# Placing the first expert slot's half steps ahead of the last routing ranks in a spectral filter and mixture-of-experts kernel

## The chip, the cores and the metric

The kernel runs on one core of a Trainium2 chip. Its time is the device time of one execution in microseconds; a median over runs is given for the kernel as a whole, and one profiled execution shows where the time goes. Engine names are those of the profile: PE (TensorE matmul) and PEld (its weight load), DVE (VectorE), ACT (ScalarE), POOL (GpSimd), SP (SyncE, which only issues DMAs here). An "ACTq" or "SPq" entry is a DMA issue by that engine's sequencer.

## The reference

Eight sequences of 2496 tokens by 256 channels are filtered in the frequency domain, and the 19968 filtered tokens go through a layer of eight experts in which each token uses one expert:

```python
X = np.fft.rfft(x, axis=1)
y = np.fft.irfft(X * (filt_r + 1j * filt_i)[None], n=2496, axis=1)    # 8 x 2496 x 256
x = y.reshape(19968, 256)
xn = x / (norm(x) + 1e-6); en = expert_emb / (norm(expert_emb) + 1e-6)
logits = xn @ en.T / tau                       # 19968 x 8
e = argmax(logits, 1); gate = softmax(logits)[e]
out = gate * (relu(x @ w1[e]) @ w2[e])         # w1: 8 x 256 x 1024, w2: 8 x 1024 x 256
```

## The kernel before

**Convolution.** Each sequence is one group. The transform of 2496 points is done as 64 by 39 with matmuls, in three stages per group: `conv_s1` (products named `s`, stored to DRAM as `SD`), `conv_s2` (loads `a` from `SD` and `f` from the filter; multiplies; product `sa`; stored as `ZD`), and `conv_sb` (product `y` from `ZD`, then the rows' logits and the routing).

**Routing.** `conv_sb` for group 0 cuts its 11 tile pairs into two chunks, of six and five. When a chunk's logits are complete, `route` runs in three parts, one per half step: part one sums the logits, part two finds the winner and the one-hot `oh`, part three computes the rank of each token within its expert by matmuls on `oh` (`rk`), adds them to the running `base`, and queues the rows' scatter to DRAM (`XS`, by indirect DMAs on POOL), sorted by expert. For group 0 alone, the first 128 rows of every expert are taken from the first chunk: the base is raised to 128 behind it, so the second chunk's rows never fall among them. The area is cleared beforehand.

**Slots.** A slot is a block of up to 256 rows of one expert. Its rows are read back from `XS` by a transposing DMA (`xTf` for the eight fixed slots of 128 rows, `xT` later), and it takes four half steps: `up(fp)` computes `ph` by 12 matmuls on PE, then ACT writes the relu `h` and DVE its low part; `down(fp)` two half steps later accumulates `po`. `read_pair(p)` reads the rows of two fixed slots, with four DMAs on SP's queue: a transposing read and a small `meta` read for each.

**Weights.** The 16 weight arrays of 1 MB are loaded by SP at the half steps in `WLOADS`. Then steps named by letter prepare each expert: `g` (sums of squares on PE, `gram`), `d` (its diagonal, DVE), `p` (sum, PE), `q` (scales, DVE), `k` (high part, ACT, line 324), `l` (low part, DVE, line 331). `WPREP` puts them at half steps of the head; `WLATE` puts the rest at the slots' own half steps, counted from 0.

**Order.** The head is one loop over half steps `n`, in which ACT, PE, DVE and SP take their instructions in the order of the program. In each step the head's own work comes first, then the weights' steps, then one slot half step if `n >= SLOTS`. For group 0, half steps 0 to 10 are `conv_s1`, 11 to 34 `conv_s2`, from 35 on `conv_sb`. The second chunk's logits end at 62, its three routing parts are at 63, 64 and 65, and its ten scatters at 65 to 69. From half step 53 on the second group's `conv_s1` runs alongside, one tile pair per half step: pair 9 at 63, pair 10, the last, at 64; its `s` products are stored by ACT's DMA queue. Behind the head the second group's `conv_s2` follows; the scheduler, which plans by a timeline of its own, may place its instructions among those of the head's last part, but behind the second chunk's new `base`, POOL's last scatter and the first `read_pair` (`behind("first")`, `behind("pl")`, `behind("read")`).

The loop itself:

```python
for n in range(HEAD):
    next(whole_head, None)
    weights(n)          # clears, read_pair(0) at FIRST_ROWS, loads, prep steps
    keep_warm(n)
    if n >= SLOTS:
        next(steps)     # one slot half step: up, late weight steps, down
```

Of the kernel before, what the change touches and what calls it, by code (L numbers as in the profile page):

```python
# [46 lines left out]
DLAG = 2  # L47
MID = 8
XNEXT = 43
WLOADS = (38, 40, 42, 44, 46, 48, 50, 52, 54, 56, 58, 60, 61, 63, 78, 79)  # L50
WPREP = {43: "g00", 44: "g01", 46: "d0", 48: "p0", 49: "q0 g10", 50: "k00", 51: "l00 k01 g11", 52: "d1 l01 k02",
# [5 lines left out]
WLATE = {16: "l52 k53 p6", 17: "l53 q6 g70", 18: "k60 g71", 19: "d7 l60 k61", 20: "l61 k62", 21: "l62 k63 p7",  # L57
         22: "l63 q7", 23: "k70", 24: "l70 k71", 25: "l71 k72", 26: "l72 k73", 27: "l73"}
SIDE = 18
CLEAR, FIRST_ROWS = 39, 64  # L60
SLOTS, HEAD = 66, 82
WARM = {-1: 8, 12: 26, 35: 22, 40: 6}
FRONT = 0
FIXED = 128
# [10 lines left out]
def moe_spectral_kernel(  # L75
# [810 lines left out]
    def read_pair(p):  # L886

        xT = mp2.tile([P, 4, 256], F16, tag="xT", name=f"xTf{p}")
        for j in range(2):
            e = 2 * p + j  # L890
            meta = mpm.tile([P, 2, 2], F32, tag="meta", name=f"metaf{e}")[:, :1]
            pairs[e] = xT[:, :, j * FIXED:(j + 1) * FIXED], meta
            at = slice(e * CAP, e * CAP + FIXED)
            read_rows(0, *pairs[e], XS16[at, 0:2 * D], XS[at, D:D + 2], fixed=True)
        last.setdefault("read", last["sp"])
# [151 lines left out]
    def weights(n):  # L1047
# [3 lines left out]
        if n == FIRST_ROWS:  # L1051
            read_pair(0)
        if n in WLOADS:
            next(loads)
# [62 lines left out]

    begun, late = [], dict(WLATE)

# [132 lines left out]
```

## Time and profile before

| | us |
|---|---|
| median of 3 runs | 1350.24 |
| lowest and highest of them | 1348.65, 1364.11 |
| the profiled execution | 1344.95 |
| its span, first to last instruction | 1343.2 |
| mean granted clock of PE | 0.970 |

The profiled execution is a little faster than the runs of the table; sums are made against its own time. Times in rows are microseconds from the span's start. A row of a timeline merges neighbouring instructions of one kind (xN). In brackets it says how long the engine was idle before, and what ended that. The releaser is inferred: the last semaphore to arrive.

### The profile page before, as it was taken

How to read it: one execution, taken by the hardware profiler on the slowest of the kernel's cores; microseconds unless marked ns; L12 is line 12 of the kernel's file. 1: busy time of each engine (PE TensorE's matmuls, PEld its weight loads, DVE VectorE, ACT ScalarE, POOL GpSimd, SP SyncE). 2: the span in 40 equal slices, each digit the busy share in tenths (PEclk: the TensorE clock that was granted, in tenths of full speed). 3: DMA queues.
4: the chain of work that ended last, by engine and by line, in shares of the span. 5: the costliest groups of instructions: out<-in, count | busy, mean ns of one | idle time of the engine just before them, and what ended most of it. 6: DMA issues, size and time to landing. Idle time of an engine off the chain costs nothing.

```text
span 1343.2 us, 36499 instructions
## 1 busy us (share of the span) xinstructions
PE 1246.3 (93%) x11027; PEld 981.2 (73%) x11027; DVE 938.8 (70%) x3078; ACT 762.2 (57%) x1760; POOL 489.2 (36%) x569
## 2 busy tenths in 40 slices
PE   7867899959897999998999999999999999999997
PEld 2344686627584778786888788878887888889886
DVE  1455796756586688976889697868786885444664
ACT  2175466825664586667757785678465843233333
POOL 0003322264255325541464346423633175111221
PEclk9997899979998999998999999999999999999999
DMA  7899868887868697868769887777675544221221
GB/s 230 271 325 369 246 185 217 186 229 226 200 169 238 190 202 174 226 192 184 168 182 245 193 195 203 224 186 194 173 196 140 119 119 106 54 49 41 57 45 37
DMA packets 272354, 241.27 MB, mean 180 GB/s; under 512 B 167123, under 2 KB 212182, under 8 KB 270373
## 3 DMA queue, kind: packets, MB, share of 16 engines
q1 hardware_dynamic: 243965, 177.87, 52.0%
q0 software_dynamic: 24320, 57.97, 14.8%
q10 hardware_dynamic: 3880, 3.03, 0.7%
q8 instruction: 104, 1.70, 0.6%
q14 instruction: 85, 0.70, 0.2%
HBM read 122.32 MB, written 85.57 MB: 155 GB/s over the span
## 4 chain that ended last, share of the span: by engine, by line
PE 71%; DMA 18%; DVE 4%; issue 3%; ACT 2%; POOL 1%; SPq 1%; ACTq 0%; DVEq 0%; POOLq 0%
PE ph L967 27%; PE po L992 26%; PE s L444 5%; DMA yT<-rows 4%; DMA f<-ZD 3%; PE sa L444 3%; PE y L444 2%; DMA f<-in_filt 2%; DMA W<-in_w 2%; PE s L439 2%; PE sa L555 2%; DMA XS<-rows,ixi 1%; DMA SD<-s 1%; PE y L439 1%; PE lp L610 1%
## 5 line engine op out<-in xcount | busy, mean ns | idle before, releaser
L992 PE MATMUL po<-W,h 128*128 (+1 forms) x3824 | 494.4, 273 | 0.2 <-ACT h L975 0.2
L967 PE MATMUL ph<-xT,wp 128*128 128x256 f16 (+2 forms) x4224 | 471.6, 258 | 10.9 <-DMA xT<-XS 3.7
L967 PEld LDWEIGHTS <-wp 128*128 128x128 f16 x4224 | 357.7, 98 | 87.8 <-issue 41.6
L992 PEld LDWEIGHTS <-h 128*128 128x128 f16 x3824 | 361.2, 98 | 68.9 <-issue 26.4
L975 ACT ACTIVATE h<-ph 128x512 f16<-128x512 f32 (+2 forms) x384 | 201.7, 527 | 244.9 <-PE ph L967 182.2
L1007 POOL DMA_INDIRECT out_dram<-o,meta x153 | 158.5, 1036 | 305.9 <-ACT o L1006 228.6
L976 DVE SCALAR_TENSOR_TENSOR h<-ph,h 128x512 f16<-128x512 f32 (+2 forms) x384 | 227.1, 591 | 48.3 <-ACT h L975 46.6
L951 DVE COPY wp<-W 128x1024 f16 x352 | 164.8, 469 | 117.8 <-PE ph L967 115.3
L790 POOL DMA_INDIRECT XS<-rows,ixi x176 | 180.1, 1023 | 142.0 <-issue 93.8
L536 POOL TENSOR_TENSOR yy<-yy,xs 128x512 f32<-128x512 f32 x60 | 80.5, 1343 | 105.6 <-DVE xs L499 85.0
L497 DVE TENSOR_TENSOR yy<-s,f 128x256 f32<-128x256 f32 x160 | 61.3, 417 | 62.5 <-ACT xs L529 27.8
L400 POOL DMA_DIRECT2D in<-in_x x66 | 38.8, 588 | 168.8 <-DVE xp L413 57.3
L635 DVE SCALAR_TENSOR_TENSOR rows<-y,rr,rows 128x256 f16<-128x256 f32 x176 | 76.7, 477 | 23.8 <-ACT rows L632 23.1
L668 ACT ACTIVATE rows<-y 128x256 f16<-128x256 f32 x176 | 67.3, 398 | 26.5 <-PE y L439 24.3
L1006 ACT ACTIVATE o<-po,meta 128x256 f32<-128x256 f32 x148 | 64.0, 478 | 28.8 <-PE po L992 27.3
L632 ACT ACTIVATE rows<-y,rr 128x256 f16<-128x256 f32 x176 | 75.5, 496 | 7.5 <-DVE rr L673 5.8
L558 ACT COPY z<-sa 128x512 f32<-128x512 f32 x80 | 46.7, 584 | 49.9 <-PE sa L555 41.2
L465 ACT COPY s<-s 128x512 f32<-128x512 f32 x88 | 52.7, 600 | 27.8 <-PE s L439 15.9
L595 ACT COPY yT<-tp 128x512 f16<-128x512 f16 x99 | 58.6, 605 | 9.1 <-PE tp L593 5.4
L444 PE MATMUL s<-xp,c1h 117*128 117x512 f32 (+1 forms) x144 | 62.0, 438 | 0.0
L412 ACT CAST yp<-yy 128x512 fp32r<-128x512 f32 x50 | 30.9, 619 | 53.0 <-POOL yy L536 52.5
L610 PEld LDWEIGHTS <-yT 128*128 128x128 f16 x704 | 33.2, 98 | 35.5 <-DMA yT<-rows 17.9
(208 smaller groups left out, 1688.8 us busy)
## 6 DMA issues: line engine op xcount, KB each, us to landing
f<-in_filt SPq DMA_DIRECT2D x160, 256.0 KB
a<-SD SPq DMA_DIRECT2D x80, 256.0 KB
ZD<-z SPq DMA_DIRECT2D x80, 256.0 KB
f<-ZD SPq DMA_DIRECT2D x80, 240.0 KB
SD<-s SPq DMA_DIRECT2D x70, 240.0 KB
in<-in_x POOLq DMA_DIRECT2D x66, 234.0 KB
W<-in_w SPq DMA_DIRECT2D x14, 1024.0 KB
in<-in_x SPq DMA_DIRECT2D x22, 234.0 KB
```

The source lines that it names most:

```text
L444: nc.tensor.matmul(out_, w[:k], b, start=(n == 0), stop=(n == 2))
L536: nc.gpsimd.tensor_tensor(out=yy, in0=yy, in1=xs, op=ALU.add)
L632: nc.scalar.activation(rows[:, i, 0:D], y[:, i], AF.Copy, scale=rr[:, u:u + 1])
L635: nc.vector.scalar_tensor_tensor(out=rows[:, i, D:2 * D], in0=y[:, i], scalar=rr[:, u:u + 1], in1=rows[:, i, 0:D], op0=ALU.mult, op1=ALU.s ...
L668: nc.scalar.activation(rows[:, i, D:2 * D], y[:, i], AF.Square, accum_out=ssq[:, u + i:u + i + 1])
L790: i = nc.gpsimd.indirect_dma_start(out=XS, out_offset=bass.IndirectOffsetOnAxis(ap=ix, axis=0), in_=src, in_offset=None)
L951: last["dve"] = nc.vector.tensor_copy(wp, src)
L967: last["pe"] = nc.tensor.matmul(ph[:, fi, :size], wp[:, k * 2 + wh, fi * P:(fi + 1) * P], xT[:, xh * 2 + k, :size], start=(c == 0), stop=( ...
L975: last["act"] = nc.scalar.activation(h[:, 0, :, :size], ph[:, :, :size], AF.Relu)
L976: last["lo"] = nc.vector.scalar_tensor_tensor(out=h[:, 1, :, :size], in0=ph[:, :, :size], scalar=0.0, in1=h[:, 0, :, :size], op0=ALU.max, ...
L992: nc.tensor.matmul(self.po[:, s], h, self.Wp[:, off + wh * 1024:off + wh * 1024 + D], start=(fp == 0 and fi == 0 and c == 0), stop=(fp == ...
L1007: i = nc.gpsimd.indirect_dma_start(out=out, out_offset=bass.IndirectOffsetOnAxis(ap=self.meta[:n, s, 0:1].bitcast(I32), axis=0), in_=o, in ...
```

## The change

Five constants and two tables. Slots' half steps begin at `n` = 63 instead of 66, the fixed rows' first read is issued at 61 instead of 64, and the head's loop ends at 79 instead of 82, so that it holds sixteen slot half steps as before. Weight loads at 60, 61 and 63 go to 59, 60 and 62, and the last two from 78 and 79 to 75 and 76. From half step 64 on the weights' steps are laid anew; the steps that no longer fall into the head open `WLATE`, which now ends at slot half step 28 instead of 27.

```diff
-WLOADS = (38, 40, 42, 44, 46, 48, 50, 52, 54, 56, 58, 60, 61, 63, 78, 79)
+WLOADS = (38, 40, 42, 44, 46, 48, 50, 52, 54, 56, 58, 59, 60, 62, 75, 76)
 WPREP = {43: "g00", 44: "g01", 46: "d0", 48: "p0", 49: "q0 g10", 50: "k00", 51: "l00 k01 g11", 52: "d1 l01 k02",
          53: "l02 k03", 54: "l03 p1 g20", 56: "q1 g21", 57: "k10", 58: "d2 l10 k11", 59: "l11 k12", 60: "l12 k13 p2",
-         61: "l13 q2 g30", 62: "k20 g31", 63: "l20", 64: "d3", 66: "k21 p3", 67: "l21 k22 q3", 68: "l22 k23 g40",
-         69: "l23 k30 g41", 70: "d4 l30 k31", 71: "l31 k32", 72: "l32 k33 p4", 73: "l33 q4 g50", 74: "k40 g51",
-         75: "d5 l40 k41", 76: "l41 k42", 77: "l42 k43 p5", 78: "l43 q5 g60", 79: "k50 g61", 80: "d6 l50 k51",
-         81: "l51 k52"}
-WLATE = {16: "l52 k53 p6", 17: "l53 q6 g70", 18: "k60 g71", 19: "d7 l60 k61", 20: "l61 k62", 21: "l62 k63 p7",
-         22: "l63 q7", 23: "k70", 24: "l70 k71", 25: "l71 k72", 26: "l72 k73", 27: "l73"}
+         61: "l13 q2 g30", 62: "k20 g31", 63: "l20", 64: "d3 k21", 65: "l21 k22 p3", 66: "l22 k23 q3", 67: "l23 g40",
+         68: "k30 g41", 69: "l30 k31 d4", 70: "l31 k32", 71: "l32 k33 p4", 72: "l33 q4 g50", 73: "k40 g51",
+         74: "d5 l40 k41", 75: "l41 k42", 76: "l42 k43 p5", 77: "l43 q5 g60", 78: "k50 g61"}
+WLATE = {16: "d6 l50 k51", 17: "l51 k52", 18: "l52 k53 p6", 19: "l53 q6 g70", 20: "k60 g71", 21: "d7 l60 k61",
+         22: "l61 k62", 23: "l62 k63 p7", 24: "l63 q7 k70", 25: "l70 k71", 26: "l71 k72", 27: "l72 k73", 28: "l73"}
-CLEAR, FIRST_ROWS = 39, 64
-SLOTS, HEAD = 66, 82
+CLEAR, FIRST_ROWS = 39, 61
+SLOTS, HEAD = 63, 79
```

## Rows read from the trace of the kernel before

**Rows 1.** The page: busy time, share of the span, instructions.
```profile
PE 1246.3 (93%) x11027; PEld 981.2 (73%) x11027; DVE 938.8 (70%) x3078; ACT 762.2 (57%) x1760; POOL 489.2 (36%) x569
```
**Rows 2.** Windows of 20 us: length, busy times, clock, DMA share, GB/s.
```profile
core 0: us, PE busy (x) PEld busy (x) DVE busy (x) ACT busy (x) POOL busy (x), PEclk, DMA share, GB/s
...
120.00:140.00 20.00, 12.59 (x78) 7.32 (x77) 10.87 (x34) 10.24 (x16) 3.52 (x3) 0.76 1.05 343
...
180.00:200.00 20.00, 20.00 (x183) 14.45 (x180) 18.34 (x63) 12.40 (x22) 4.14 (x3) 1.00 0.61 177
```
**Rows 3.** Timeline of PE, 133 to 152: start, length, what, idle time before.
```profile
133.48 2.13 PE L439 MATMUL s<-in,c_sb 117*128 117x512 f32 x6
141.03 0.23 PE L753 MATMUL rk<-oh,lt 128*128 128x80 f16 x1 [5.43 <-DVE oh L743]
...
141.85 2.72 PE L967 MATMUL ph<-xTf,W 128*128 128x128 f16 x24
...
148.66 1.93 PE L439 MATMUL s<-a,c_sb 128*128 128x512 f32 x4
150.43 0.83 PE L967 MATMUL ph<-xTf,W 128*128 128x128 f16 x12
151.10 0.82 PE L992 MATMUL po<-W,h 128*128 128x256 f16 x6
```
**Rows 4.** Small windows around the first slot, columns as in rows 2.
```profile
141.03:147.20 6.17, 5.99 (x66) 5.91 (x66) 4.62 (x20) 3.42 (x6) 2.09 (x2) 0.53 0.91 281
131.00:135.60 4.60, 4.21 (x32) 2.50 (x33) 0.92 (x4) 1.41 (x3) 0.00 (x0) 1.00 1.06 387
138.00:140.00 2.00, 0.00 (x0) 0.00 (x0) 1.73 (x4) 1.23 (x3) 0.00 (x0) 0.99 0.88 212
```
**Rows 5.** Timeline of DVE, 138 to 146.
```profile
138.20 1.28 DVE L331 SCALAR_TENSOR_TENSOR W<-W,wsc 128x1024 f16<-128x1024 f32 x1 [4.47 <-ACT W L324]
...
145.33 0.42 DVE L976 SCALAR_TENSOR_TENSOR h<-ph,h 128x256 f16<-128x256 f32 x1 [1.24 <-ACT h L975]
```
**Rows 6.** Timeline of ACT, 136 to 138.
```profile
136.65 0.32 ACTq L467 DMA_DIRECT2D SD<-s  x1
137.02 1.15 ACT L324 ACTIVATE W<-W,wsc 128x1024 f16<-128x1024 f32 x1 [3.88 <-DMA SD<-s]
```
**Rows 7.** The chain that ended last, three pieces: start, length, what.
```profile
125.71 10.87 DMA SD<-s
...
145.18 2.90 DMA a<-SD
...
295.77 3.44 DMA xT<-XS
```
**Rows 8.** SP's DMA issues, 125 to 138.
```profile
125.44 0.89 SPq L264 DMA_DIRECT2D W<-in_w  x2
130.53 1.34 SPq L878 DMA_TRANSPOSE xTf<-XS  x1
...
136.96 0.33 SPq L879 DMA_DIRECT2D metaf<-XS  x1
137.74 1.19 SPq L878 DMA_TRANSPOSE xTf<-XS  x1
```
**Rows 9.** SP's waits, 85 to 150: us in total, times, longest.
```profile
SPq L878 <- DMA XS<-rows,ixi: 4.1, 1, 4.1
...
SPq L879 <- DMA W<-in_w: 1.3, 1, 1.3
...
SPq L878 <- DMA xTf<-XS: 0.4, 1, 0.4
```
**Rows 10.** PE's waits, 140 to 225, columns as in rows 9.
```profile
PE ph L967 <- DVE h L976: 0.5, 1, 0.5
```
**Rows 11.** PE's waits, 225 to 305, columns as in rows 9.
```profile
PE s L439 <- DMA a<-SD: 6.0, 1, 6.0
PE sa L555 <- POOL yy L536: 4.7, 1, 4.7
...
PE ph L967 <- DMA xT<-XS: 1.6, 1, 1.6
```

## The prediction, made before the changed kernel was seen

> **What bounds the kernel now.** I read the page first: its busy line says that PE works 93% of the span [rows 1], so what counts is PE time: idle PE, and PE at its low clock. The windows of 20 us say where early on [rows 2]: from 120 to 140 PE is busy for 12.6 us of 20, with the DMA engines full (share 1.05, 343 GB/s) and the clock down to 0.76; from 180 to 200 it is busy for all 20 at full clock. The reader is to see two regimes: a head that lives on DMA, and, right behind it, a stretch in which PE is the limit.
>
> The first slot starts at their border, so the key view is PE's order around it [rows 3]: the last products of the head end at about 135.6, then PE stands 5.43 us for `oh`, the operand of the second chunk's rank matmuls (`rk`, 141.03), and only behind these come the first slot's `ph` matmuls (141.85). In code: half steps 63 and 64 hold the two last `s` products, 65 the ranks, 66 the first `up`. The small windows of the same place [rows 4] show the second loss: behind that gap the granted clock averages 0.53 for 6.17 us, so of its two levels it is mostly the 1.2 GHz one.
>
> Why is `oh` late? Go back through the engines: DVE stops 4.47 us for one weight `low` (138.20) [rows 5], which waits for the `high` at 137.02, which stands on ACT behind a store's issue at 136.65 [rows 6]; the chain names a store issued at 125.71 that took 10.87 us as what held that issue [rows 7]. So the chunk's ranks are late because DMA is full, not because of the slot.
>
> The slot's read has a time of its own: SP waited 4.1 us for the first chunk's scattered rows [rows 9] and issued the first transposing read at 130.53; two loads of 1 MB went out on the same queue from 125.44 [rows 8].
>
> **The change, part by part.**
>
> *(a) Three half steps sooner.* Sixteen slot half steps lie in the head before and after, so no work is added or removed; `up(0)` and `up(1)` now stand ahead of `rk` in PE's order, while the third stays behind it (at half step 65 the head's own work goes first). If the rows are there, 24 `ph` matmuls move into the 5.43 us gap. At full clock a dozen take 0.67 us from start to start (150.43 to 151.10 [rows 3]), so two dozens are 1.34 us, and the gap holds them four times over. Behind the ranks they are gone.
>
> What this is worth depends on the clock. In the gap it was still 0.99 from 138 to 140, and 0.53 from 141 on [rows 4]: it fell near the gap's end. With two dozens in it, 5.43 − 1.34 = 4.1 us of idle time are left at most, and in pieces. Low bound: the clock falls all the same, and the dozens give back what they cost there, 24 in 2.72 us [rows 3]: 2.7. High bound: it doesn't fall; 6.17 us at 0.53 are 3.3 us of full-clock work, less 1.34 leaves 1.9 us in place of 6.2: 4.2. I take 3.9, near the high end, since the row from 138 to 140 is nearest.
>
> *(b) What the moved steps put ahead of the ranks elsewhere.* On DVE the `h` low part (0.42 [rows 5]), on ACT a relu of the same tile, which I estimate at as much, each once or twice in front of parts two and three of `route`. DVE is idle 4.47 us just there, which covers most; behind the late `low` nothing is covered. From 0 to 0.42 + 0.42 = 0.8; I take 0.5. What is queued behind: `oh`, `rk`, the new base and the scatters, for which the second group's rows and the later slots wait.
>
> *(c) The read at half step 61 instead of 64, one weight load now behind it.* The last three loads of the first run move from half steps 60, 61, 63 to 59, 60, 62. So the read has 1 MB less in front, and that load now stands on SP behind the read's own wait: it goes out near 134 instead of 125.9, and behind it on SP are the second pair's read and the second group's first `f` loads, which one issue (0.89 us for two [rows 8]) pushes by 0.4. At the 387 GB/s of 131 to 135.6 [rows 4] 1 MB is 2.7 us. The read, and the store that blocks ACT, can come from 0 to 2.7 us sooner. Against that, the same bytes come back in front of the `a` load that lands at 148.08 [rows 7], up to 2.7 us of it. I count nothing: gain and return are of one size.
>
> *(d) Weights' steps.* Against the slots' own count they fall one or two half steps later; five more of them (`d6 l50 k51 l51 k52`) lie behind step 16. Two `low` are 2.6 us of DVE, by 1.28 each [rows 5]; in absolute time they stay about where they were, since the slots came forward. The nearest deadlines: slot 5's `l51` at step 17, used at 20; slot 7's `l71` at step 26, used at 28. Zero, covered by those two or three half steps; but DVE is 92% busy from 180 to 200 [rows 2], and uncovered it is 2.6 us.
>
> The sum against the profiled execution's 1344.95 us: −3.9 + 0.5 = −3.4, so 1341.5. That execution lies 5.3 us under the median shown, 1350.24; the forecast for a median is 1346.8, say **1347**.
>
> Does it reach the end? From 142 to 225 PE's longest wait is 0.5 us [rows 10], so what is gained at 141 is carried to there. At the first handover to full slots PE waits for `a` (6.0), `yy` (4.7) and `xT` (1.6) [rows 11]; each hangs on work that PE paced before, so it shifts as a whole. That is the weak point: behind the head the order is planned, and a shift can make those waits longer or shorter.
>
> **The rivals.**
>
> *The gain is handed back (1350).* The second group's first product starts at 148.66 [rows 3], its operand landed at 148.08 [rows 7]; a PE that is 4 us ahead could just wait for it, as that load does not come sooner by the slot. For it: DMA is full until then. Against it: the slots' matmuls have their data and can stand ahead of it.
>
> *The read lands late and holds the ranks: slower (1354).* PE takes its work in order, and `up(0)` now stands in front of the last `s` product and of `rk`. If the rows land at T, `rk` is reached at T + 1.3 (two dozens) + 1.1 (half of the last 2.13 us of products [rows 3]). It costs from T = 141.0 − 2.4 = 138.6 on. Bounds for T: a later transposing read landed in 3.44 us [rows 7], which gives 134.0; by the 10.87 us of the store in this very stretch it is 141.4. Then `rk` is 2.8 us late, and the last `s` product's store about 4, for which the `a` load waits: 4 us in all, 1354. The rows against my forecast: SP's fourth read was released by an earlier read only at 137.74, and a load was still awaited until 136.96 [rows 8, 9]. For it: the load less ahead, 2.7 us, which would put the same event at 135.
>
> The Trainium skill says, in "DMA: Bandwidth & Descriptors", section "Queues, rings and completion order", that on each DMA engine the descriptors of one queue are taken in ring order. That rule speaks for the late read: the rows lie behind whatever loads SP has sent. The trace agrees as far as those two waits go; no run here has timed the first read alone. By the rule the load that moved behind the read counts in full, and T is about 135.
>
> *The handover falls out otherwise.* If the waits of 6.0, 4.7 and 1.6 us [rows 11] shrink or grow by most of themselves, that is 9 to 12 us: about 1336 at one end, about 1358 at the other.
>
> **How the numbers follow.** Forecast (1344 to 1348) 0.42; handed back (1348 to 1352) 0.28; late read (1352 to 1357) 0.15; handover shorter (1333 to 1343) 0.09; longer (over 1357) 0.06. The range goes from 1334 to 1357: low, the forecast and one handover's waits; high, the late read with the uncovered `low`. Two per cent, about what a measurement of this kernel can tell from no change, is 27 us; no case reaches it. Faster 0.02, same 0.95, slower 0.03: the tails are for a plan that falls out quite differently.
>
> **What would show it.** Right: in the changed profile 24 `ph` matmuls start between 133 and 140, ahead of `rk`; `rk` is at 141.5 or sooner; no 5 us without PE there; granted clock over 0.8 from 141 to 147; the first product on `a` no later than 148.7. Wrong: PE waits for the transposing read over 3 us ahead of `rk` (late read); idle PE just ahead of the first product on `a` (handed back); the first full slot starts as late as before although the first slot started 7 us sooner (lost at the handover).

## The result, and the profile after

The changed kernel takes 1359.91 us (median of 20 runs, 1352.73 to 1367.76), the kernel before beside it 1350.48 us (20 runs, 1347.40 to 1364.11). The ratio is 1.0059, interval 1.0042 to 1.0076: slower by 0.6%, some 8 us (by the two medians alone 9.4). The forecast was 1347, so the sign was wrong too. The two profiled executions lie further apart than the medians: spans of 1360.3 and 1343.2 us.

The lines that answer to [rows 1 to 11], in the same order. The page's busy line: PE has 7 us more of work in a span 17 us longer.

```profile
PE 1253.5 (92%) x11027; PEld 984.0 (72%) x11027; DVE 938.5 (69%) x3078; ACT 762.5 (56%) x1760; POOL 489.7 (36%) x569
```

Windows of the kernel after, columns as in [rows 2]: two slices of 20 us, and three small ones around the first slot. Behind the ranks the clock averages 0.55 as it did before (0.53, [rows 4]).

```profile
120.00:140.00 20.00, 12.96 (x84) 8.06 (x84) 11.66 (x33) 9.88 (x15) 3.55 (x4) 0.66 1.05 342
180.00:200.00 20.00, 20.00 (x204) 15.21 (x202) 18.00 (x61) 12.87 (x21) 3.19 (x3) 1.00 0.51 156
145.28:151.45 6.17, 5.99 (x56) 5.27 (x56) 5.84 (x21) 3.75 (x8) 1.61 (x2) 0.55 0.60 186
138.00:140.00 2.00, 2.00 (x17) 1.27 (x16) 1.03 (x1) 1.41 (x2) 0.00 (x0) 1.00 1.00 389
141.00:145.00 4.00, 0.22 (x4) 0.10 (x2) 1.52 (x7) 1.24 (x3) 0.00 (x0) 0.88 0.98 298
```

The timeline of PE, as in [rows 3]. The two dozens of `ph` do stand ahead of the ranks (138.49, 140.37) and waited for no read, but `rk` is at 145.28 instead of 141.03, behind a wait for `oh` of 4.06 us, and the first product on `a` at 151.95 instead of 148.66. The head's last products end at 140.4 instead of 135.6: before any slot step PE had stood 3.79 us for ACT's copy of `s` (132.06).

```profile
132.06 0.59 PE L592 MATMUL tp<-ident,rows 128*128 128x128 f16 x4 [3.79 <-ACT s L464]
...
138.49 0.84 PE L966 MATMUL ph<-xTf,W 128*128 128x128 f16 x12
139.16 1.28 PE L438 MATMUL s<-in,c_sb 117*128 117x256 f32 x4
140.37 0.84 PE L966 MATMUL ph<-xTf,W 128*128 128x128 f16 x12
145.28 0.23 PE L752 MATMUL rk<-oh,lt 128*128 128x80 f16 x1 [4.06 <-DVE oh L742]
...
151.95 1.93 PE L438 MATMUL s<-a,c_sb 128*128 128x512 f32 x4
```

Why `oh` is late: first ACT, then DVE (timelines, as in [rows 5, 6]). ACT issues a store at 142.52, after 3.48 us for a small read of the second pair of slots, `metaf`; the slot's relu stands behind that store, DVE's low part of `h` behind the relu (143.31), and `route`'s second part behind the low part (143.65).

```profile
138.84 0.57 ACT L464 COPY s<-s 128x512 f32<-128x512 f32 x1
142.52 0.32 ACTq L466 DMA_DIRECT2D SD<-s  x1
142.89 0.38 ACT L974 ACTIVATE h<-ph 128x256 f16<-128x256 f32 x1 [3.48 <-DMA metaf<-XS]
```

```profile
143.31 0.42 DVE L975 SCALAR_TENSOR_TENSOR h<-ph,h 128x256 f16<-128x256 f32 x1 [3.06 <-ACT h L974]
143.65 0.23 DVE L731 TENSOR_REDUCE mx<-l 128x10 f32<-128x80 f32 x1
...
144.99 0.24 DVE L742 TENSOR_TENSOR oh<-w,mv 128x80 f16<-128x80 f32 x1
```

SP's issues and waits and a piece of the chain, as in [rows 7 to 9]: the first transposing read still goes out at 131.53 (130.53 before), as SP waited 5.4 us for the scattered rows (4.1 before).

```profile
131.53 1.31 SPq L877 DMA_TRANSPOSE xTf<-XS  x1
132.91 0.56 SPq L878 DMA_DIRECT2D metaf<-XS  x1
...
137.80 0.33 SPq L878 DMA_DIRECT2D metaf<-XS  x1
```

```profile
SPq L877 <- DMA XS<-rows,ixi: 5.4, 1, 5.4
```

```profile
131.53 6.25 DMA xTf<-XS
```

All that is 3 to 4 us by 152. PE's waits, as in [rows 10, 11]: behind that of the ranks none over 0.8 us follows up to 225; then two loads of the second group's last stage cost more, `lp` for the transposed rows `yT` 5.6 and `y` for `f` 2.9, where they were 2.6 and 1.4; and behind that stage, at the handover to full slots, the waits for `a` and `yy` together are 12.5 us (10.7 before). First the changed kernel, then the two of the kernel before that [rows 11] leave out.

```profile
PE s L438 <- PE ph L966: 0.8, 1, 0.8
```

```profile
PE sa L554 <- POOL yy L535: 7.6, 1, 7.6
PE lp L609 <- DMA yT<-rows: 5.6, 3, 2.3
PE s L438 <- DMA a<-SD: 4.9, 1, 4.9
PE y L438 <- DMA f<-ZD: 2.9, 1, 2.9
```

```profile
PE lp L610 <- DMA yT<-rows: 2.6, 3, 1.5
...
PE y L439 <- DMA f<-ZD: 1.4, 1, 1.4
```

Where does it show in time? The second group's three chunks each end in a rank. Timeline of PE, the stage's first `y` product and those matmuls, first of the kernel before, then of the changed one:

```profile
225.89 1.12 PE L439 MATMUL y<-f,csb_sb 120*128 120x512 f32 x2 [1.41 <-DMA f<-ZD]
...
257.17 0.19 PE L753 MATMUL rk<-oh,lt 128*128 128x64 f16 x1
...
270.73 0.19 PE L753 MATMUL rk<-oh,lt 128*128 128x64 f16 x1
...
276.10 0.20 PE L753 MATMUL rk<-oh,lt 128*128 128x48 f16 x1 [1.04 <-DVE oh L743]
```

```profile
229.42 2.08 PE L438 MATMUL y<-f,csb_sb 120*128 120x512 f32 x2 [2.90 <-DMA f<-ZD]
...
257.47 0.19 PE L752 MATMUL rk<-oh,lt 128*128 128x64 f16 x1
...
279.88 0.26 PE L752 MATMUL rk<-oh,lt 128*128 128x64 f16 x1
...
285.02 0.20 PE L752 MATMUL rk<-oh,lt 128*128 128x48 f16 x1 [0.49 <-DVE oh L742]
```

The first chunk's rank is 0.3 us late, the third's 8.9. The first looks better than it is. Counted in the program's order, 44 slot half steps stand on PE ahead of that rank before the change and 41.7 after (528 and 500 `ph` matmuls, twelve to a half step); at full clock a half step is 1.33 us, by these two pieces of the changed kernel's chain, so 3.1 us of slot work now lie behind it.

```profile
171.37 0.67 PE ph L966 x12
172.04 0.66 PE po L991 x6
```

That fits the first `y` product of the stage, which was at 225.89 and is at 229.42. So about 3.5 us come before 230, and of the 5.4 us that follow, the two waits named above are 4.5 (8.5 less 4.0). Behind this group the instructions of PE, DVE, ACT and SP stand in the same order again, but for a few neighbours that change places on DVE and SP, and the first chunks' ranks of the later groups are 6.6 to 17.4 us late in these two traces, which lie further apart than the medians. Two traces from one chip show it more cleanly, e11, the changed kernel again, and e12, which takes the time of the kernel before (both below, spans of 1360.1 and 1354.2 us): there the changed kernel's first rank is 2.2 us sooner (258.24), its third 6.8 us later (285.87), and the end 6 us later.

### The profile page after: what moved, and what is told of

Its sections match the earlier page's. It is cut to its first block, busy times and chain, and to the rows that moved or that the text cites. A ratio compares the mean times of both kernels' runs of the same rounds, so it can differ in the third digit from the quotient of the medians.

```text
span 1360.3 us, 36499 instructions
## 1 busy us (share of the span) xinstructions
PE 1253.5 (92%) x11027; PEld 984.0 (72%) x11027; DVE 938.5 (69%) x3078; ACT 762.5 (56%) x1760; POOL 489.7 (36%) x569
## 4 chain that ended last, share of the span: by engine, by line
PE 67%; DMA 14%; DVE 3%; issue 3%; ACT 2%; SPq 1%; POOL 1%; DVEq 0%; POOLq 0%; ACTq 0%
PE ph L966 25%; PE po L991 25%; PE s L443 5%; DMA yT<-rows 4%; PE y L443 3%; PE sa L443 2%; PE s L438 2%; DMA f<-ZD 2%; DMA XS<-rows,ixi 2%; PE sa L554 2%; DMA f<-in_filt 1%; DMA a<-SD 1%; PE y L438 1%; PE tp L592 1%; PE lp L609 1%
## 5 line engine op out<-in xcount | busy, mean ns | idle before, releaser
L966 PE MATMUL ph<-xT,wp 128*128 128x256 f16 (+2 forms) x4224 | 477.5, 260 | 11.3 <-DMA xT<-XS 4.6
L975 DVE SCALAR_TENSOR_TENSOR h<-ph,h 128x512 f16<-128x512 f32 (+2 forms) x384 | 227.4, 592 | 52.4 <-ACT h L974 50.8
L496 DVE TENSOR_TENSOR yy<-s,f 128x256 f32<-128x256 f32 x160 | 61.5, 418 | 61.4 <-ACT xs L528 24.0
L443 PE MATMUL s<-xp,c1h 117*128 117x512 f32 (+1 forms) x144 | 61.5, 434 | 0.0
```

What stands on the lines that cost most here:

```text
L443: nc.tensor.matmul(out_, w[:k], b, start=(n == 0), stop=(n == 2))
L966: last["pe"] = nc.tensor.matmul(ph[:, fi, :size], wp[:, k * 2 + wh, fi * P:(fi + 1) * P], xT[:, xh * 2 + k, :size], start=(c == 0), stop=( ...
L975: last["lo"] = nc.vector.scalar_tensor_tensor(out=h[:, 1, :, :size], in0=ph[:, :, :size], scalar=0.0, in1=h[:, 0, :, :size], op0=ALU.max, ...
```

## The experiments

Two theories were told apart in the end. **A** (its later form is A2): the slot in front of the ranks costs it, by the held store, the relu and low part behind it, and ranks 4 us late. **G**: the re-laid tables cost it; they move the second group's last stage against the slots. Where an expectation carries another letter, it is a guess held at that time and told there. The runs came on four chips. On one (e10 to e13) the kernel before took 1354 us; on the others 1476 to 1486 us, with a lower granted clock (0.93 instead of 0.97) and, in the kernels with the old order that have a trace there (e1, e2, e6), already 22 to 23.5 us from the first to the second of those ranks, the stretch that the expectations call from first to last. Each ratio is to the kernel before on the same chip.

**The parts of the change, one by one, on the kernel before.**

```diff
 e1  WLOADS = (..., 58, 59, 60, 62, 78, 79)
 e2  CLEAR, FIRST_ROWS = 39, 61
 e3  WPREP, WLATE = the re-laid tables
```

> The kernel before with three weight loads one half step sooner (60, 61, 63 become 59, 60, 62) and nothing else. Theory A (the ranks come 4 us late because a store of the second group waits, on ACT, for the second pair's small read, and the slot's relu and its low part stand between): none of that is here, so 0, within 2 us of the kernel before, ranks' first matmul near 141. Rival B (the loads that go out sooner fill the DMA engines ahead of the stores of pairs 6 to 8; in the changed profile the product of pair 8 starts at 134.2 instead of 131.4): slower by 3 to 5 us, the product of pair 8 at about 134, the ranks near 144.

> The kernel before with the first pair's read issued at half step 61 instead of 64; slots, loads and weights' steps as before, so one load waits on SP behind the read. Theory A: no relu of a slot stands ahead of the ranks and the second pair is read at its old place, so 0, within 2 us. Rival C (the read itself, or the load held up behind it, is what costs): slower by 4 us or more, with a wait for that load or a later first product on the second group's data.

> The kernel before with the weights' steps of the changed kernel (both tables), slots, read and loads as before. Theory A: 0, within 2 us, since the steps stay off PE's path. Rival D (the re-laid steps, now nearer to their use and more of them behind slot half step 16, hold DVE or ACT in the stretch where PE is the limit): slower by 4 to 9 us, with PE waits on DVE or ACT between 150 and 300.

Measured: 1.0025 (0.9994 to 1.0055), 1.0009 (0.9981 to 1.0036) and 1.0007 (0.9974 to 1.0039). None differs from the kernel before by itself, as far as these intervals go.

**The change with the old loads**, `WLOADS` at 60, 61, 63 again (the last two stay at 75 and 76):

> The changed kernel with the three weight loads back at half steps 60, 61 and 63. Theory A: still slower than the kernel before by 6 to 10 us, ranks at 144 or later, with the relu of the first slot held behind a store on ACT. Rival B (loads): most of the loss is gone, within 4 us of the kernel before.

Measured: 1.0061 (1.0031 to 1.0090). So the loss is there without the moved loads, and it is there on a chip on which the kernel before takes 9% longer.

**The relu taken from in front of the ranks.** In e5 the relu and low part of the first two half steps are issued behind the ranks, at half step 65; in e9 the weight step `k20`, `l20` as well, for which those up to half step 73 are laid anew once more. e6 moves that weight step alone, on the kernel before.

```diff
+            if run["hold"]:
+                held.append(relu)
+            else:
+                relu()
...
+            run["hold"] = n < 65
+            while held and not run["hold"]:
+                held.pop(0)()
```

> The changed kernel, but the relu and low part of the first two slot half steps are issued behind the second chunk's ranks (at half step 65) instead of at 63 and 64; the matmuls stay ahead of the ranks. Theory A (relu behind a held store on ACT, its low part ahead of part two of the routing on DVE): the DVE row ahead of part two is the weight's low part again, the ranks come 3 to 8 us sooner than with the change, and the time is within 3 us of the kernel before or below it, 0.0 to 0.3% faster. Rival E (it is the matmuls ahead of the ranks, or the read's place, whatever the relu does): as slow as the changed kernel, 0.5 to 0.7% over the kernel before.

> The changed kernel with the relu and low part of its first two half steps behind the ranks and the weight piece's steps (k20, l20) behind them too. Theory A: nothing on DVE stands ahead of part two any more; PE's wait ahead of the ranks is under 1.5 us and the time is below the kernel before by 2 to 6 us (0.15 to 0.45%). Rival: as e5, no better, since the second group's data comes no sooner.

> The kernel before with one weight piece's high and low step (k20, l20) moved from half steps 62 and 63 to 65 and 66, behind the ranks; nothing else. Where the late low part (138.2 in the profile before, behind a held store on ACT) is what makes the one-hot late, the ranks come 4 to 5 us sooner, PE's wait ahead of them falls from 5.4 to under 1.5, and the kernel is 3 to 5 us faster (0.2 to 0.4%). Rival: the ranks come sooner but the exponent behind the same store holds the new base and the first product on the second group's data, which stays where it is: 0, within 2 us.

Measured: e5 1.0049 (1.0020 to 1.0078), e9 1.0043 (1.0013 to 1.0072), e6 1.0017 (0.9982 to 1.0052). With no relu and no low part ahead of `oh` most of the loss stays; theory A had wanted it gone. A blemish: the third half step of the slot now waits for the late low part, 4.6 us in e5, and the first product on `a` falls back to 166.91 in e5 and 162.72 in e9 (152.36 in e1, on the same chip), so this alone did not settle it. In e6 the ranks do come sooner (140.10, 143.54 in e1), but PE then stands 5.9 us in front of a weight step (`gram`, for `wmax`) and the time doesn't fall.

**The slots one half step sooner instead of three, none ahead of the ranks**, `SLOTS, HEAD = 65, 81`:

> The changed kernel with the slots' half steps from 65 on instead of 63 (head's end at 81): loads, read and weights' tables as changed, but no slot step stands ahead of the ranks. Theory A: the loss is gone, within 3 us of the kernel before. Rival F (the three half steps are not it; loads, read and weights' steps together, each within its error alone, make the sum): still 0.4 to 0.6% slower.

Measured: 1.0084 (1.0054 to 1.0114). A smaller move with the same tables is no cheaper, and the loss is there with no slot step ahead of the ranks (144.24; the first `ph` at 145.85): against theory A.

**The store that ACT held.** The stores of the second group's pairs 8 to 10 go out on POOL's queue, on either kernel; beside them the changed kernel once more and the changed kernel without the moved slots.

```diff
-                (nc.scalar if g == 1 else nc.sync).dma_start(m, st[:k, h])
+                (nc.gpsimd if g == 1 and t >= 8 else nc.scalar if g == 1 else nc.sync).dma_start(m, st[:k, h])
```

> The kernel before, but the stores of the second group's last three pairs (8 to 10) are issued by POOL, which is idle there, instead of ACT. Where stores held on ACT set the ranks and the second group's start: ACT no longer stands for them, the ranks come 3 to 5 us sooner, the loads of a 2 to 4 us sooner, and the time is 0.2 to 0.4% under the kernel before. Where they do not set the end: within 0.15%.

> The changed kernel with the same three pairs' stores issued by POOL. Theory A2 (a store held on ACT behind the second pair's small read, with the slot's relu behind it and the second group's loads waiting for it): the loss is gone, from 0.3% under the kernel before to 0.15% over it, PE's wait ahead of the ranks under 3 us and the loads of a at 145 or sooner on a chip like the first. Rival F: still 0.4 to 0.8% over.

> The changed kernel itself once more, so that the others of this set have it beside them on one chip. All theories: 0.4 to 0.8% over the kernel before, as in the first comparison (0.59%).

Measured: e12 0.9997 (0.9970 to 1.0024), e13 1.0053 (1.0019 to 1.0086), e11 1.0062 (1.0038 to 1.0086). Timeline of PE in e12, the ranks again; its first `y` product is at 231.96, 6 us later than before the change, and yet the third rank is only 3 us late and the time is the same:

```profile
260.48 0.19 PE L753 MATMUL rk<-oh,lt 128*128 128x64 f16 x1
...
274.22 0.19 PE L753 MATMUL rk<-oh,lt 128*128 128x64 f16 x1
...
279.07 0.22 PE L753 MATMUL rk<-oh,lt 128*128 128x48 f16 x1 [1.04 <-DVE oh L743]
```

In e13, with the new tables, first and second rank are 19.2 us apart again (13.7 in e12), although no wait for `metaf` is left on ACT. Nor is PE's wait for `oh` more than 0.53 us, as A2 had it; yet the second chunk's ranks are at 145.69, 3.7 us behind e12's (142.02). PE had stood 4.89 us at 135.71 for ACT's copy of `s`, which waited for an earlier store: with one wait gone, the one ahead of it sets the time.

```profile
135.71 0.59 PE L592 MATMUL tp<-ident,rows 128*128 128x128 f16 x4 [4.89 <-ACT s L464]
...
145.69 0.20 PE L752 MATMUL rk<-oh,lt 128*128 128x80 f16 x1 [0.53 <-DVE oh L742]
...
261.59 0.19 PE L752 MATMUL rk<-oh,lt 128*128 128x64 f16 x1
...
280.82 0.19 PE L752 MATMUL rk<-oh,lt 128*128 128x64 f16 x1
```

So the held store isn't the cause of the loss, and being some 5 us late at 150 or at 230 isn't a loss by itself.

**Everything but the moved slots**, `SLOTS, HEAD = 66, 82`. In e10 the last two loads stay at 75, 76; e15 puts them back to 78, 79.

> The changed kernel with the slots' half steps back at 66 and the head's end at 82: loads, read and weights' tables as changed, slots as before. Rival F (loads, read and weights' tables together make the loss, whatever the slots do): 0.4 to 0.9% over the kernel before, as much as the changed kernel beside it. Theory A2 (the slots' steps are needed for the loss): within 0.25% of the kernel before and at least 0.3% under the changed one.

> The changed kernel with the slot's own steps back behind the second chunk's ranks and the head's last loads at the half steps they had before; the new tables and the sooner read stay. Theory G: the loss stays, 1.004 to 1.009, with 19 to 23 us from the second group's first rank to its last. Rival A2: 0.998 to 1.002.

Measured: e10 1.0129 (1.0088 to 1.0170); e15 1.0052 (1.0014 to 1.0090). e10 has a fault of its own: with the old start of the slots, its last loads go out at 143.97, ahead of the second group's `f` (SP's timeline), and the first product on `a` follows at 157.25.

```profile
143.97 2.81 SPq L270 DMA_DIRECT2D wraw<-in_w  x4
146.83 2.68 SPq L485 DMA_DIRECT2D f<-in_filt  x4
```

e15 is the clean form: the loss is there in full with the slots where they were. That is against A2.

**The tables moved, not re-laid.** e17 and e18 are one kernel: the change, but each weight step from half step 64 on comes three half steps sooner, as the slots do, and what shares a half step is as before; `WLATE` is that of the kernel before. e14 is the opposite: the change, with the weight steps at their old half steps, so that `WLATE` begins seven steps earlier in the list.

```diff
 e17  61: "l13 q2 g30", 62: "k20 g31", 63: "l20 d3 k21 p3", 64: "l21 k22 q3", ... 78: "l51 k52"}
      WLATE = {16: "l52 k53 p6", ... 27: "l73"}
 e14  63: "l20", 64: "d3", 66: "k21 p3", 67: "l21 k22 q3", ... 78: "l43 q5 g60"}
      WLATE = {16: "k50 g61", 17: "d6 l50 k51", ... 29: "l73"}
```

> The changed kernel with every step of the tables of weights' steps moved by three half steps, as the slot's steps were, instead of re-laid: which step shares a half step with which is again as before, only three sooner. In PE's order the first rank of the second group's last chunks but one then stands behind 44 slot half steps again, as before the change (41.7 in the changed kernel). Theory G (the re-laid tables let the second group's convolutions pass the slots, and their transposing loads lie bare at 257 to 280 us): the loss is gone, 0.995 to 1.002 of the kernel before, and the stretch from the group's first rank to its last falls from 22 us to about 14. Rival A2 (the slot in front of the ranks, with the held store, costs it by itself): 1.004 to 1.008.

> The changed kernel with the weights' steps moved by three half steps with the slot's steps instead of re-laid, once more. It took 1.001 of the kernel before where that took 1486 us, against 1.005 to 1.010 of the kernels with other tables beside it. Theory G: on a chip on which the kernel before takes about 1350 us, 0.996 to 1.002, and 13 to 16 us from the second group's first rank to its last instead of the 22.4 us of the changed kernel; on the slower chip 0.999 to 1.003 again. Rival A2 (the moved slot and its held store cost it): 1.004 to 1.008 where the kernel before takes 1350 us.

> The changed kernel with the weights' steps at the half steps they had before, so that they come three later against the slot than before the change. In PE's order the second group's first rank of the last chunks stands behind 41 slot half steps, still sooner than before the change (44). Theory G, which goes by that place: 1.003 to 1.009. If instead the re-laid tables cost by which steps share a half step: 0.998 to 1.002. Rival A2: 1.004 to 1.008, with the second chunk's ranks still 4 us late at 145 us.

Measured: e17 1.0010 (0.9978 to 1.0043), e18 1.0002 (0.9974 to 1.0030), e14 1.0103 (1.0062 to 1.0145). The loss goes with the tables, and not with which weight steps share a half step: in e14 they share as before the change. On one chip the medians are 1487 us for e17, 1496 for e15 and 1505 for e14, where the kernel before takes 1486. The changed kernel as it is did not run on the chips of e17 and e18; nearest to it on such a chip is e4, 1.0061. The stretch that was to shrink to 14 us did not: it is 24.1 us in e18, and e1, e2 and e6 have 22 to 23.5 us on such a chip. In e18 everything that A2 blames is there and worse. ACT's timeline: the store's wait for `metaf` is 4.27 us; PE's: the ranks stand at 151.01, 10 us later than in the trace of the kernel before ([rows 3]), 7.5 later than in e1 (143.5), which is on a chip as slow, and 3.7 later than in e19 (147.3) on the same chip; and the time is that of the kernel before.

```profile
147.59 1.15 ACT L324 ACTIVATE W<-W,wsc 128x1024 f16<-128x1024 f32 x1 [4.27 <-DMA metaf<-XS]
```

```profile
151.01 0.22 PE L753 MATMUL rk<-oh,lt 128*128 128x80 f16 x1 [1.03 <-DVE oh L743]
```

**The tables alone, twice more.**

> The kernel before with the re-laid tables of weights' steps alone, as in the earlier run of this edit, in which the kernel before took 1477 us and already had 22 us in the stretch in question. Theory G: where the kernel before takes about 1350 us and has 13.6 us there, 1.004 to 1.007; where it takes 1477 us, 1.000 to 1.002 as then. Rival A2: 0.998 to 1.002 on either.

> The kernel before with the re-laid tables of weights' steps alone, beside the kernel above on the same chip. Theory G, tables alone: 1.004 to 1.007 where the kernel before takes about 1350 us, with 19 to 23 us from the second group's first rank to its last (13.6 us before); 1.001 to 1.004 where it takes 1480 us. If the tables cost only together with another part of the change: 0.998 to 1.002. Rival A2: 0.998 to 1.002.

Measured: 1.0036 (0.9996 to 1.0076) and 1.0035 (1.0010 to 1.0059), after 1.0007 for the same edit in e3. By themselves the tables measure 0.26% in the mean of the three, with one interval clear of 1. The whole 0.6% is not theirs alone on these chips. What is missing came with the loads, the read and the slots beside them; but e17 and e18 hold all of these and lose nothing, so they would cost only together with the re-laid tables, and the runs don't divide it. Neither the tables alone nor e17 ran on a chip of the faster kind.

PE's waits from 225 to 305 set side by side, of e18 (tables moved) and e19 (tables re-laid), which ran on one chip: 3.6 us for `y` and `lp` against 6.2. The third rank is no later in e19, though (291.85, 292.87 in e18), and the two profiled executions took the same time (1476.86 us in e18, 1476.55 in e19): by themselves these waits don't show the loss on this chip.

```profile
PE y L439 <- DMA f<-ZD: 2.1, 1, 2.1
...
PE lp L610 <- DMA yT<-rows: 1.5, 1, 1.5
```

```profile
PE lp L609 <- DMA yT<-rows: 3.6, 2, 2.2
PE y L438 <- DMA f<-ZD: 2.6, 1, 2.6
```

It shows just behind that window, at the handover. In all kernels the same number of PE's matmuls stands ahead of the first `ph` of a full slot, and from the third rank up to it in the same order, so there they can be compared. In e19 the first rank is 1.7 us sooner than in e18 and this `ph` 4.2 us later: PE stood 5.38 us between the products on `a` for DVE's `xs`, where it stood 0.54 in e18. Timeline of PE, e18, then e19:

```profile
316.75 2.34 PE L967 MATMUL ph<-xT,wp 128*128 128x256 f16 x20 [1.67 <-DMA xT<-XS]
```

```profile
308.25 2.04 PE L438 MATMUL s<-a,c_sb 128*128 128x512 f32 x2 [5.38 <-DVE xs L498]
...
320.93 2.29 PE L966 MATMUL ph<-xT,wp 128*128 128x256 f16 x10 [3.43 <-DMA xT<-XS]
```

**All kernels by one number.** The number is how many slot half steps stand, in PE's program order, ahead of the second group's first rank; beside it the ratios, the sum of the waits for `yT` and `f` between 225 and 305 us, and the time from that rank to the first `ph` of a full slot, on the chips on which the kernel before takes about 1350 us and on those on which it takes about 1480:

| half steps ahead | kernels | ratios | waits, us | to the full slot, us |
|---|---|---|---|---|
| 44 | before, e1, e2, e6, e12, e17, e18 | 0.9997 to 1.0025 | 2.2 to 4.4 | at 1350: 42.1, 42.6; at 1480: 50.4 to 52.4 |
| 43 | e5, e9 | 1.0049, 1.0043 | 3.6, 4.5 | at 1480: 53.1, 51.8 |
| 41.7 | after, e3, e4, e8, e10, e11, e13, e15, e16, e19 | 1.0007 to 1.0129 | 5.5 to 9.4 | at 1350: 47.7 to 51.5; at 1480: 56.2 to 61.5 |
| 41 | e14 | 1.0103 | 8.5 | at 1480: 60.1 |

Every kernel at 44 is like the one before; of the others only e3 and e16 have an interval that touches 1. The place goes with `WLATE`: none of its steps added (44), five added (41.7, or 43 where the relu is late as well), seven added (41). The last column parts the kernels at 44 and at 41.7 on either kind of chip by 3.8 us and more, of which 3.1 are the slot work that now stands behind the first rank. At 1350 us the rest lies between the first rank and the third, at 1480 for the larger part behind the third, in the wait at the handover. That the place in the order is what costs, by the loads left bare behind it, is argued from these waits; they don't explain e5 and e9, which are late ahead of that rank.

The planned order differs behind the first full slot as well. There PE's matmuls stand as in the kernel before in the changed kernel, e4, e5, e9 and e11 to e14; in a second order in e6, e10, e17 and e18; in a third in e2, e8 and e15; in a fourth in e1, e3, e16 and e19. Within each of the first three the kernels at 44 are at most 0.2% over the kernel before and all others 0.4% or more. In the fourth, e1, at 44, has 1.0025 without the tables, so what the tables cost alone can't be told from what that later order costs.

The re-laid tables are shown to be the part of the change without which no loss was seen; by which stretch of the order they cost the whole 8 us stays open in part. No kernel beat the one before.

## Why the prediction was wrong

*What bounds the kernel* held: PE at 92 to 93% of the span, and a fast full regime behind 150.

*(a)*, the 24 `ph` into the gap, held as to place: they start at 138.49 and 140.37, and no 5 us without PE follow them. The gain didn't come. The idle stretch moved behind them (4.06 us), and the clock fell behind that one in the same way (0.55). I had reckoned the wait for `oh` as fixed in time and asked only what fits into it.

*(b)* is the term of the sum that was mis-sized at this place: 0.5 taken, 0 to 0.8 as bounds, 4.25 us measured at `rk`. The bounds held the durations of relu and low part (0.38 and 0.42, as estimated); what they left out is that the relu stands on ACT behind a store, which can be held: 3.48 us for a read that I had in the list of moved DMAs and had followed only on SP's own queue. Not all of the 4.25 is this term's: PE came late to the ranks as well, its last products of the head ending 4.8 us later, and in e13, without the hold, the ranks are still 3.7 us behind e12's. No term of the sum had that delay, and no run takes it apart.

*(c)*, the sooner read at nothing: the read went out 1.0 us later, not sooner, and landed in time. The rival *late read* did not occur: PE never waited for the rows.

So at 152 the sum was wrong by 6.7 us (3.3 late where 3.4 sooner was forecast). Yet this is not what made the kernel slower. e18 has those ranks later still and takes 1.0002; e12 is 5 us late at the first product on `a` (153.65) and takes 0.9997 of the kernel before. *Does it reach the end?* was answered yes, from PE's short waits up to 225; the right answer was no, for a gain as for a loss. At the handover PE waits over 10 us for transfers and POOL, and those waits take up a few microseconds in either direction.

*(d)* is the step that failed: "Zero, covered by those two or three half steps". I asked of each weight step only whether its deadline was met, and the deadlines were met. Five steps more behind step 16, which I named and priced at nothing, go with another order of the second group's last stage against the slots, and the re-laid tables alone measure 0.35% twice and 0.07% once, up to 5 us; with the steps moved rigidly the whole change costs nothing (1.0010 and 1.0002).

The rival *the handover falls out otherwise* was the one that came true, at its longer end: 1358 was its time and 1359.91 the result, with a chance of 0.06. It had the place nearly right, but the waits it listed (`a`, `yy`, `xT`) went from 12.3 us to 12.7 together (4.9, 7.6 and 0.24); those that grew, by 4.5, are for `yT` and `f`, one stage earlier. On the slower chips the handover itself did grow: from the third rank to the first full slot e17 and e18 take 24 us, the kernels at 41.7 between 27 and 30. Its cause was thought to be a plain shift; the runs point to the order instead. *Handed back* names what happens to the slot's own move: no gain at 225. The range, ending at 1357, missed by 3 us because that chance was priced too low for a change that rewrites a table from which the order behind the head is planned.

## What to carry to other kernels

Where part of the order is planned by a program, an edit's first effect is the new order: compare the two orders over the whole span, and count what work stands ahead of each long transfer, before pricing single steps. When a step of several parts is moved, move what is laid against it rigidly first, and re-lay it in a second change; the two are then measured apart. And an issue on an engine's queue can be held by another engine's transfer, so all that stands behind a store is as late as the worst of these.

## What the runs showed of the hardware

A store on ACT waited for a read that SP had issued. In the traces that store and the read `metaf` count on one completion counter (the read issued at 137.80 and the store at 142.52 in the changed kernel); SP's and ACT's transfers there take turns on a few such counters. ACT stood 3.48 us in the changed kernel, in front of a relu that had its data, and 4.27 us in e18. The read is small and yet came some 4.7 us after its issue (137.80 to 142.5), in a stretch with the DMA engines at a share of about 1.

The same kernel took 1350 to 1354 us on some chips and 1476 to 1486 us on others, 9 to 10% more, at a granted clock of 0.93 instead of 0.97; a loss of 0.6% was found on both kinds.
